# Two memsets moved behind the warm matmuls at the start of an attention and feed-forward kernel

## The chip, the cores and the metric

One core of a Trainium2 chip runs the whole program. The metric is the device time of one execution in microseconds. Before the change it is 955.84 us in the median of three runs (953.73 to 956.58); the profiled execution took 955.52 us.

## The reference

Three stages follow each other on 4 batches, 8 heads, 576 positions and a head width of 64; q, k, v and the output are float32, the weights 64-bit floats:

```
scores = q k^T / 8 + ALiBi bias, only where 0 <= i - j < 128
attn   = softmax(scores) v                 -> x [2304, 512]
x      = ((x w_a) * (x w_b)) w_out         (inner width 1536)
out    = ((x w1) * (x w2)) w3 w_out2       (inner width 1024)
```

The window of 128 means that a block of 128 query rows needs only its own block of keys and the one before it.

## The kernel before

The feed-forward products need float32 accuracy. Each factor is split into two `fp32r` parts, high and low (`hi` and `lo`), and three products (`lo` by `hi`, `hi` by `lo`, `hi` by `hi`) are summed in PSUM. The weights are loaded as pairs of integers (`raw`) and converted: ScalarE takes the absolute value of the upper word (`L113`, into `ca`) and a function of the lower word (`L116`, into `ce`), VectorE does four passes with shifts and masks (`L120`, `L123`, `L127`, `L132`), then `split` writes the high part on ScalarE (`L141`) and the low part on VectorE (`L78`). One such chain converts a block of 128 x 512 weights.

Attention runs in steps of one batch, one run of query blocks (blocks 0 and 1, blocks 2 and 3, block 4) and one pair of heads. For each block, `prep` transposes q and k on TensorE (`L287`, PSUM tiles `tr`) and ScalarE copies them out (`L296` into `w_q` and `w_k`, `L302` into `last_q` and `last_k`). A step then has: the scores (`L341`, tiles `s`), bias and row minimum on VectorE (`L368`, tile `pe`), the exponential on ScalarE (`L374`), the transposition of the weights (`L406`) and its copy (`L273` on ScalarE, `L275` on VectorE, tile `pt`), the product with v (`L428`), the division (`L434`, `L450`, `L452`) and the split of the result into `x_hi` (`L457`, ScalarE) and `x_lo` (VectorE). The four head pairs of the first run complete `x` for the first 256 tokens: four `x_hi`, the fourth for the last head pair.

In the gaps of attention, a `Filler` places the first feed-forward products (`g1`, matmuls at `L589`). Their first group needs the first 256 tokens of `x` and the first converted weight blocks. The conversions themselves are handed out one stage at a time by `side.turn()`.

What sets the order: TensorE's instructions are written by hand from the attention loop on (`manual_schedule` for PE). The instructions of the other engines, and TensorE's before that loop, are put in order when the program is built, by a simulated timeline (`schedule_with_timeline_sim=True`). Each engine works through its own list in order and waits at the first instruction whose inputs are missing. All loads are issued by SyncE's queue; the order of its first entries is: q and k of block 0, q and k of block 1, v twice, q and k of block 2 (`early`), further q, k and v, then the first two blocks of w_a and w_b.

At the start VectorE clears `last_q` and `last_k` (`L794`, `L795`), then in `consts` the tiles `pad`, `q_last` and `k_t`, and last `warm` (`L811`), a tile of zeros on which ten matmuls without use run (`keep_warm`, `L396`). `last_q` and `last_k` hold the last, half block of q and k of batch 0; their cleared parts are read by the scores of that block.

Of the kernel before, what the change touches and what calls it, by code (L numbers as in the profile page):

```python
# [44 lines left out]
def attention_moe_moe(ctx, tc, q, k, v, w_a, w_b, w_o, w_1, w_2, w_3, w_o2, out):  # L45
    nc = tc.nc
# [3 lines left out]
    P = 128  # L50
# [3 lines left out]
    LAST = S - (NB - 1) * P  # L54
# [337 lines left out]
    def keep_warm(cnt, x):  # L392

        ps = mm_tile(W)
        for y in range(cnt):
            nc.tensor.matmul(ps[:, :x.shape[1]], x[:, 0:P], x, start=(y == 0), stop=(y == cnt - 1))  # L396
# [69 lines left out]
    def mm_tile(n):  # L466
        ps = pools["mm"]
        turn[0] += 1
        return ps[turn[0] % len(ps)].tile([P, n], F32, name="mm")
# [321 lines left out]
    ys = ExitStack()  # L791
    y_p = ys.enter_context(tc.tile_pool(name="y_p", bufs=1, side="right"))
    last_t = [y_p.tile([P, NP, (1 + x) * P], F32, name=f"last_{'qk'[x]}") for x in range(2)]
    nc.vector.memset(last_t[0], 0.0)  # L794
    nc.vector.memset(last_t[1][:, :, P + LAST:], 0.0)  # L795
    pools["gate"] = gate_pa
    pools.update(abufs=1, gbufs=2)

# [11 lines left out]
    fl = Filler()  # L810
    nc.vector.memset(warm, 0.0)  # L811
    keep_warm(10, warm[:, 0:2 * P])
    paid = 0.0
    fixed = ExitStack()
    fixed.enter_context(tc.manual_schedule(engines={mybir.EngineType.PE}))
# [65 lines left out]
```

## Time and profile before

| | |
|---|---|
| median of three runs | 955.84 us |
| profiled execution | 955.52 us |
| its span, first to last instruction | 953.7 us |
| TensorE matmuls busy | 935.6 us |
| VectorE busy | 541.0 us |
| ScalarE busy | 421.7 us |
| mean granted TensorE clock | 0.996 |

The span is what the trace covers; the execution's own time is 1.8 us longer. The averages hide that the first 44 us look different from the rest: in a row of busy time by stretch, each engine's busy time stands behind the length of the stretch, and the granted clock of TensorE near the end (1.00 is 2.4 GHz, 0.50 is 1.2 GHz). In the rows of a timeline an instruction's duration reaches a little into the next one of the same engine, because the engine overlaps the end of one with the start of the next.

### The profile page before, as it was taken

The page shows a single profiled execution, that of the slowest core. Times are in us where ns is not written, and L with a number is a line of the kernel's source. Part 1 is how long each engine was busy: PE and PEld are TensorE (multiplying, and loading weights), DVE is VectorE, ACT ScalarE, POOL GpSimd, SP SyncE. Part 2 cuts the span into 40 slices and gives each one's busy share as a digit, 9 for nine tenths or more (in the row PEclk, how much of TensorE's full clock was granted, in tenths as well). Part 3 has the DMA queues.
Part 4 walks back from the last instruction along what each step waited for, and adds up shares of the span by engine and source line. Part 5 has one row for each costly group of instructions (what it writes and reads, how often), then busy time and mean ns, then how long its engine had stood idle before and what let it go on. Part 6 is the DMA issues. An engine that isn't in the chain of part 4 may idle for free.

```text
span 953.7 us, 13991 instructions
## 1 busy us (share of the span) xinstructions
PE 935.6 (98%) x5350; PEld 782.4 (82%) x5350; DVE 541.0 (57%) x1283; ACT 421.7 (44%) x952; POOL 157.8 (17%) x139
## 2 busy tenths in 40 slices
PE   7899999999999999999999999999999999999998
PEld 5687878878888888888888888888888888888886
DVE  5979787837995456675735744813822822522222
ACT  6978787845753245344524432433421411311111
POOL 3000000011112111120111111355211112111111
PEclk9999999999999999999999999999999999999999
DMA  9633333004441223132412320300300300000112
GB/s 231 140 79 73 80 72 73 2 1 154 134 133 56 89 94 105 67 121 79 152 36 78 122 67 17 117 1 1 118 15 1 126 7 1 23 1 1 44 59 97
DMA packets 90371, 68.28 MB, mean 72 GB/s; under 512 B 58304, under 2 KB 79296, under 8 KB 90304
## 3 DMA queue, kind: packets, MB, share of 16 engines
q1 hardware_dynamic: 90304, 67.38, 24.6%
q8 instruction: 42, 0.69, 0.3%
q14 instruction: 25, 0.20, 0.1%
HBM read 58.20 MB, written 8.91 MB: 70 GB/s over the span
## 4 chain that ended last, share of the span: by engine, by line
PE 92%; DVE 4%; ACT 3%; issue 1%; DMA 0%; POOL 0%; DVEq 0%
PE mm L589 51%; PE mm L641 13%; PE mm L657 10%; PE mm L493 5%; PE tr L428 3%; PE s L341 2%; PE mm L617 2%; PE tr L406 2%; ACT pe L374 2%; PE tr L287 2%; DVE pe L368 1%; DVE pe L388 1%; PE mm L485 1%; PE mm L629 1%; DMA early<-in_q 0%
## 5 line engine op out<-in xcount | busy, mean ns | idle before, releaser
L78 POOL TENSOR_TENSOR gl<-g,gh 128x512 fp32r<-128x512 f32 (+1 forms) x102 | 125.2, 1228 | 779.2 <-ACT gh L601 779.2
L598 DVE TENSOR_TENSOR g<-a,mm 128x512 f32<-128x512 f32 (+1 forms) x102 | 63.4, 621 | 201.9 <-PE mm L589 200.9
L601 ACT ACTIVATE gh<-g 128x512 fp32r<-128x512 f32 (+1 forms) x102 | 59.0, 579 | 149.2 <-DVE g L598 148.8
L596 ACT ACTIVATE a<-mm 128x512 f32<-128x512 f32 (+1 forms) x102 | 55.2, 542 | 121.5 <-PE mm L589 121.5
L589 PE MATMUL mm<-x_hi,wlA 128*128 128x512 f32 (+1 forms) x416 | 102.9, 369 | 2.8 <-ACT x_hi L457 2.8
L589 PE MATMUL mm<-x_lo,whA 128*128 128x512 f32 (+1 forms) x416 | 100.2, 363 | 0.1
L589 PE MATMUL mm<-x_hi,whA 128*128 128x512 f32 (+1 forms) x416 | 100.0, 363 | 0.0
L589 PE MATMUL mm<-x_lo,whB 128*128 128x512 f32 (+1 forms) x400 | 98.7, 368 | 0.0
L589 PE MATMUL mm<-x_hi,wlB 128*128 128x512 f32 (+1 forms) x400 | 98.6, 368 | 0.0
L589 PE MATMUL mm<-x_hi,whB 128*128 128x512 f32 (+1 forms) x400 | 98.1, 368 | 0.0
L116 ACT ACTIVATE ce<-raw,pad 128x512 int32<-128x512 uint32 x76 | 57.8, 761 | 64.8 <-DVE ca L132 32.1
L589 PEld LDWEIGHTS mm<-x_hi,wlA 128*128 128x128 f32 x416 | 71.6, 190 | 15.3 <-ACT x_hi L457 3.0
L589 PEld LDWEIGHTS mm<-x_lo,whA 128*128 128x128 f32 x416 | 73.0, 190 | 12.5 <-DVE x_lo L78 0.3
L589 PEld LDWEIGHTS mm<-x_hi,whA 128*128 128x128 f32 x416 | 73.3, 191 | 12.0
L589 PEld LDWEIGHTS mm<-x_hi,wlB 128*128 128x128 f32 x400 | 71.2, 188 | 12.7
L589 PEld LDWEIGHTS mm<-x_lo,whB 128*128 128x128 f32 x400 | 71.1, 189 | 12.5
L589 PEld LDWEIGHTS mm<-x_hi,whB 128*128 128x128 f32 x400 | 71.0, 189 | 12.5
L645 DVE TENSOR_TENSOR acc<-acc,mm 128x512 f32<-128x512 f32 (+1 forms) x100 | 62.0, 629 | 32.9 <-PE mm L641 32.7
L374 ACT ACTIVATE pe<-pe,st 128x256 f32<-128x256 f32 (+1 forms) x144 | 68.5, 478 | 12.2 <-DVE st L368 11.6
L113 ACT ACTIVATE ca<-raw 128x512 f32<-128x512 f32 x76 | 50.8, 668 | 51.5 <-DMA raw<-in_moe_w 24.8
L132 DVE SCALAR_TENSOR_TENSOR ca<-ce,ca 128x512 int32<-128x512 int32 x76 | 56.3, 740 | 12.0 <-ACT ce L116 10.2
L127 DVE SCALAR_TENSOR_TENSOR ca<-raw,ca 128x512 int32<-128x512 int32 x76 | 60.9, 802 | 1.8
(137 smaller groups left out, 1543.9 us busy)
## 6 DMA issues: line engine op xcount, KB each, us to landing
raw<-in_moe_w SPq DMA_DIRECT2D x32, 512.0 KB, 3.6
raw<-in_moe_w_out SPq DMA_DIRECT2D x20, 512.0 KB, 3.5
raw<-in_moe_w_a SPq DMA_DIRECT2D x12, 512.0 KB, 3.6
raw<-in_moe_w_b SPq DMA_DIRECT2D x12, 512.0 KB, 3.6
out<-acc SPq DMA_DIRECT2D x18, 256.0 KB, 2.0
v<-in_v SPq DMA_DIRECT2D x16, 256.0 KB, 4.0
w<-ce SPq DMA_DIRECT2D x16, 256.0 KB, 2.0
raw<-w SPq DMA_DIRECT2D x16, 256.0 KB, 2.8
```

What stands on the lines that cost most here:

```text
L78: eng.tensor_tensor(out=out, in0=a, in1=b, op=ALU.subtract)
L116: nc.scalar.activation(e, lw, ACTF.Relu, bias=seven, scale=-(2.0 ** -29))
L127: nc.vector.scalar_tensor_tensor(out=ai, in0=hw, scalar=-(1 << 30), in1=ai, op0=ALU.bitwise_and, op1=ALU.bitwise_or)
L132: nc.vector.scalar_tensor_tensor(out=ai, in0=es[0], scalar=7, in1=ai, op0=ALU.bitwise_xor, op1=ALU.bitwise_or)
L374: nc.scalar.activation(pe[:, j, :n], pe[:, j, :n], ACTF.Exp, bias=st[:, 0, j:j + 1], scale=-1.0, accum_out=st[:, 1, j:j + 1],)
L589: nc.tensor.matmul(p, w[:, z, kk, :], x[:, kk], start=(y == 0), stop=(y == len(terms) - 1))
L596: nc.scalar.activation(a, ps[0], ACTF.Copy)
L598: nc.vector.tensor_tensor(out=gg, in0=a, in1=ps[1], op=ALU.mult)
L601: nc.scalar.activation(gh, gg, ACTF.Copy)
L641: nc.tensor.matmul(p, w, x, start=(y == 0), stop=(y == len(terms) - 1))
L645: nc.vector.tensor_tensor(out=ya, in0=ya, in1=p, op=ALU.add)
L657: nc.tensor.matmul(p, x, w, start=(y == 0), stop=(y == len(terms) - 1))
```

## The change

The two memsets of `last_q` and `last_k` stand in the text behind the memset of `warm` and the ten warm matmuls, instead of ahead of `consts`.

```
     last_t = [y_p.tile([P, NP, (1 + x) * P], F32, name=f"last_{'qk'[x]}") for x in range(2)]
-    nc.vector.memset(last_t[0], 0.0)
-    nc.vector.memset(last_t[1][:, :, P + LAST:], 0.0)
     pools["gate"] = gate_pa
...
     nc.vector.memset(warm, 0.0)
     keep_warm(10, warm[:, 0:2 * P])
+    nc.vector.memset(last_t[0], 0.0)
+    nc.vector.memset(last_t[1][:, :, P + LAST:], 0.0)
     paid = 0.0
```

Line numbers after the change: `warm` is cleared at `L809`, the two tiles at `L811` and `L812`; all other lines named here keep theirs. The built order changes on TensorE at the start, on VectorE and ScalarE over their first 130 and 83 rows, and on SyncE in one place, where the first load of w_out is issued one entry sooner, ahead of a q load. GpSimd's order is the same, and behind these rows nothing is moved.

TensorE, at the start of the program; `tr` are the transposed q and k, `warm` is the tile of zeros:

```order
 L877 UNCONDITIONAL_BRANCH
-L287 MATMUL tr<-ident,early 128x128 x4
 L396 LDWEIGHTS warm
 L396 MATMUL mm<-warm 128x256
```

```order
 L396 LDWEIGHTS warm
 L396 MATMUL mm<-warm 128x256
-L287 MATMUL tr<-ident,early 128x128 x12
+L287 MATMUL tr<-ident,early 128x128 x16
 L341 MATMUL s<-w_k,w_q 128x128 x2
 L341 MATMUL s<-w_k,w_q 128x256 x2
```

The four transposes of the first tile have moved behind the ten warm matmuls, to the other twelve.

ScalarE, in the third and fourth steps of attention, before the change; `raw_241`, `raw_243` and `raw_247` are the first block of w_a, the first of w_b and the second of w_a, `DMAHW4_49` to `DMAHW6_49` their loads:

```order
L374 ACTIVATE pe_329,st_328<-pe_329,st_328 128x128 [waits DVE_49]
L374 ACTIVATE pe_334,st_328<-pe_334,st_328 128x256 [waits DVE_49]
L450 ACTIVATE r_389<-tr_339 128x256 [waits PE_49]
L296 ACTIVATE w_q_116<-tr_354 128x4x128 [waits PE_49]
L273 ACTIVATE pt_371<-tr_366 128x512 [waits PE_49]
L457 ACTIVATE x_hi_67<-y_391 128x256 [waits DVE_49]
L113 ACTIVATE ca_251<-raw_241 128x512 [waits DMAHW4_49]
L116 ACTIVATE ce_253<-raw_241,pad_73 128x512
L374 ACTIVATE pe_403,st_402<-pe_403,st_402 128x128 [waits DVE_49,Activation_49]
```

The same place with the change:

```order
L374 ACTIVATE pe_329,st_328<-pe_329,st_328 128x128 [waits DVE_49]
L113 ACTIVATE ca_251<-raw_241 128x512 [waits DMAHW4_49]
L116 ACTIVATE ce_253<-raw_241,pad_73 128x512
L374 ACTIVATE pe_334,st_328<-pe_334,st_328 128x256 [waits DVE_49]
L450 ACTIVATE r_389<-tr_339 128x256 [waits PE_49]
L296 ACTIVATE w_q_116<-tr_354 128x4x128 [waits PE_49]
L113 ACTIVATE ca_260<-raw_243 128x512 [waits DMAHW5_49]
L273 ACTIVATE pt_371<-tr_366 128x512 [waits PE_49]
L113 ACTIVATE ca_311<-raw_247 128x512 [waits DMAHW6_49,Pool_49]
L457 ACTIVATE x_hi_67<-y_391 128x256 [waits DVE_49]
L374 ACTIVATE pe_403,st_402<-pe_403,st_402 128x128 [waits DVE_49,Activation_49]
```

The conversions of three weight blocks begin five to eight rows sooner, ahead of an exponential, of `r` and of the first `x_hi`.

ScalarE, around the fourth `x_hi` (`x_hi_67<-y_605`), before the change; `raw_258` and `raw_309` are the two blocks of w_out, `pe_617` and `pe_622` belong to the next step:

```order
L457 ACTIVATE x_hi_67<-y_605 128x256
L374 ACTIVATE pe_617,st_616<-pe_617,st_616 128x256
L113 ACTIVATE ca_385<-raw_258 128x512
L374 ACTIVATE pe_622,st_616<-pe_622,st_616 128x256
L374 ACTIVATE pe_617,st_616<-pe_617,st_616 128x256
L374 ACTIVATE pe_622,st_616<-pe_622,st_616 128x256
L116 ACTIVATE ce_387<-raw_258,pad_73 128x512
L141 ACTIVATE whA1_245<-ca_376 128x512
L113 ACTIVATE ca_451<-raw_309 128x512
```

With the change:

```order
L273 ACTIVATE pt_590<-tr_585 128x512
L113 ACTIVATE ca_451<-raw_309 128x512
L116 ACTIVATE ce_387<-raw_258,pad_73 128x512
L141 ACTIVATE whA1_245<-ca_376 128x512
L374 ACTIVATE pe_617,st_616<-pe_617,st_616 128x256
L374 ACTIVATE pe_622,st_616<-pe_622,st_616 128x256
L457 ACTIVATE x_hi_67<-y_605 128x256
L374 ACTIVATE pe_617,st_616<-pe_617,st_616 128x256
L374 ACTIVATE pe_622,st_616<-pe_622,st_616 128x256
```

Five instructions that stood behind the fourth `x_hi` now stand right ahead of it; the sixth, `L113` on `raw_258`, stands ten rows further up.

## Rows read from the trace of the kernel before

**Rows 1.** The page's first part: busy time of each engine.

```profile
PE 935.6 (98%) x5350; PEld 782.4 (82%) x5350; DVE 541.0 (57%) x1283; ACT 421.7 (44%) x952; POOL 157.8 (17%) x139
```

**Rows 2.** Busy time in four stretches, then granted clock, DMA share, GB/s.

```profile
core 0: us, PE busy (x) PEld busy (x) DVE busy (x) ACT busy (x) POOL busy (x), PEclk, DMA share, GB/s
14.00:38.00 24.00, 19.72 (x177) 13.33 (x176) 21.04 (x84) 23.94 (x73) 0.00 (x0) 1.00 1.09 256
36.00:38.00 2.00, 0.32 (x2) 0.32 (x3) 2.00 (x9) 2.00 (x6) 0.00 (x0) 1.00 0.83 139
38.50:42.00 3.50, 3.48 (x16) 3.48 (x17) 2.96 (x7) 3.50 (x11) 0.00 (x0) 0.51 0.00 1
44.00:64.00 20.00, 20.00 (x216) 17.01 (x214) 14.29 (x49) 16.03 (x44) 1.46 (x2) 1.00 0.35 74
```

**Rows 3.** Timeline at the fourth x_hi: start, duration, engine, line, idle and releaser.

```profile
37.23 0.40 ACT L457 ACTIVATE x_hi<-y 128x256 fp32r<-128x256 f32 x1
...
37.69 0.39 PE L589 MATMUL mm<-x_hi,wlA 128*128 128x256 f32 x1 [2.77 <-ACT x_hi L457]
```

**Rows 4.** TensorE's waits over the span: us in total, times, longest.

```profile
PE tr L406 <- DVE pe L388: 2.6, 2, 1.7
```

**Rows 5.** Timeline of VectorE at the start.

```profile
0.90 0.48 DVE L794 MEMSET last_q<- 128x512 f32 x1 [0.90 <-PEq L868]
1.38 0.27 DVE L795 MEMSET last_k<- 128x256 f32 x1
...
3.32 0.27 DVE L811 MEMSET warm<- 128x256 uint32 x1
```

**Rows 6.** Timeline of TensorE from 4 to 12 us.

```profile
4.22 1.09 PE L287 MATMUL tr<-ident,early 128*128 128x128 f32 x4 [4.22 <-DMA early<-in_q]
5.10 2.34 PE L396 MATMUL mm<-warm 128*128 128x256 f16 x10
7.24 1.78 PE L287 MATMUL tr<-ident,early 128*128 128x128 f32 x12
...
11.41 0.63 PE L287 MATMUL tr<-ident,early 128*128 128x128 f32 x4 [0.90 <-DMA early<-in_q]
```

**Rows 7.** Timeline of SyncE's queue: when four of the loads are issued.

```profile
2.87 0.89 SPq L252 DMA_DIRECT2D early<-in_k  x1
...
6.15 1.14 SPq L252 DMA_DIRECT2D early<-in_q  x1
...
13.43 0.61 SPq L88 DMA_DIRECT2D raw<-in_moe_w_a  x1
...
14.64 0.52 SPq L88 DMA_DIRECT2D raw<-in_moe_w_a  x1
```

**Rows 8.** The same four loads: KB each, us from issue to landing.

```profile
early<-in_k SPq DMA_DIRECT2D x1, 256.0 KB, 4.8
...
early<-in_q SPq DMA_DIRECT2D x1, 256.0 KB, 5.1
...
raw<-in_moe_w_a SPq DMA_DIRECT2D x1, 512.0 KB, 5.0
...
raw<-in_moe_w_a SPq DMA_DIRECT2D x1, 512.0 KB, 8.3
```

**Rows 9.** Timeline of ScalarE: exponentials and conversions.

```profile
17.53 0.50 ACT L374 ACTIVATE pe<-pe,st 128x256 f32<-128x256 f32 x1
...
18.03 0.37 ACT L450 ACTIVATE r<-tr 128x256 f32<-128x256 f32 x1
18.29 0.59 ACT L296 ACTIVATE w_q<-tr 128x512 f32<-128x512 f32 x1
18.77 0.59 ACT L273 ACTIVATE pt<-tr 128x512 f32<-128x512 f32 x1
...
19.55 0.68 ACT L113 ACTIVATE ca<-raw 128x512 f32<-128x512 f32 x1
20.12 0.77 ACT L116 ACTIVATE ce<-raw,pad 128x512 int32<-128x512 uint32 x1
...
26.05 0.64 ACT L141 ACTIVATE whA<-ca 128x512 fp32r<-128x512 f32 x1
```

More of the change, by code (lines that the diff above doesn't have):

```diff
@@ L793, in attention_moe_moe @@
     last_t = [y_p.tile([P, NP, (1 + x) * P], F32, name=f"last_{'qk'[x]}") for x in range(2)]
-    nc.vector.memset(last_t[0], 0.0)
-    nc.vector.memset(last_t[1][:, :, P + LAST:], 0.0)
     pools["gate"] = gate_pa
@@ L812, in attention_moe_moe @@
     keep_warm(10, warm[:, 0:2 * P])
+    nc.vector.memset(last_t[0], 0.0)
+    nc.vector.memset(last_t[1][:, :, P + LAST:], 0.0)
     paid = 0.0
```

## Prediction

> **What bounds the kernel now.** I read the page's totals first, then busy time by stretch, then the rows around the largest wait that is not a load, then the start. TensorE is busy in 98% of the span [rows 1], and from 44 to 64 us it has no gap at all [rows 2]: there only its own work counts, and whatever shifts its start of that stretch shifts the end. Before 42 us it is different. From 14 to 38 ScalarE is busy in 23.94 of 24 us and VectorE in 21.04; in 36:38 both are full, and TensorE has 0.32 us of work [rows 2]. So this front belongs to two engines that are full and work in order, and to loads. What ends it is the fourth `x_hi` (`L457`, the one of the last head pair) at 37.23: with it the first 256 tokens of the feed-forward input are complete, and the matmul that waited 2.77 us for it starts at 37.69 [rows 3].
>
> **The change part by part.** *The two memsets* take 0.48 and 0.27 us [rows 5]. The instructions stay, now after `warm`. VectorE is through with its memsets at 3.59, the scores that it works on next need transposes that end at 7.24 + 1.78 = 9.02 [rows 5, 6], and so they cost nothing in the new place.
>
> *TensorE's start.* `warm` was ready at 3.32 + 0.27 = 3.59; without 0.75 us in front of it, it is ready at 2.84 [rows 5]. The ten warm matmuls take 7.24 - 5.10 = 2.14 us [rows 6] and end near 5.0, where before four transposes ran first from 4.22 and the other twelve from 7.24. But transposes need loads: the fourth tile is issued at 2.87 and lands 4.8 later, at 7.67 [rows 7, 8]. Before, its transposes ended at 9.02. Now they start no sooner than 7.67 and need 0.88 us at the pace of the first four (5.10 - 4.22 [rows 6]) or half of that: they end at 8.1 to 8.6, 0.4 to 0.9 us earlier. The Trainium skill (TensorE: Matmul & The Clock Gate, What's actually happening) says that the array starts throttled and that activity releases it. By that rule the earlier warm block brings the shorter figure, 0.9. The sum is the same by either.
>
> What becomes of the 0.4 to 0.9 us? The next transposes wait for the fifth tile, issued at 6.15 and landed 5.1 later, at 11.25; TensorE already waits 0.90 us for it and goes on at 11.41 [rows 6 to 8]. Those loads wait for nothing that the change moves, so TensorE just waits longer. I take 0; the lower end is -0.9, if all of it got through.
>
> *The order behind it.* The larger part is not in the diff. ScalarE's and VectorE's instructions are ordered by a simulated timeline, and it moves the weight conversions forward. ScalarE's order shows two places; its distances from start to start are read in [rows 9]: `L374` on 256 columns 0.50, `L450` 0.26, `L296` 0.48, `L113` 0.57, and with a duration less the 0.11 by which such rows overlap the next (19.55 + 0.68 against 20.12) `L273` 0.48, `L116` 0.66, `L141` 0.53.
>
> First place: the `L113` and `L116` on `raw_241` (the first block of w_a) stood behind the exponentials of the third step, `r`, `w_q`, `pt` and the first `x_hi`. Now they stand ahead of the last of those exponentials. Their load is issued at 13.43 and lands 5.0 later, at 18.43 [rows 7, 8]. ScalarE got to that exponential at 17.53 [rows 9]. Being in order it stands for 18.43 - 17.53 = 0.90 us, with work behind it that was ready. If the head start above reaches it, it stands longer by as much; the instruction starts at 18.43 either way. So the front hangs on a load that the change does not move.
>
> Second place: from 18.43 ScalarE does `L113` 0.57, `L116` 0.66, `L374` 0.50, `L450` 0.26, `L296` 0.48, a second `L113` 0.57, `L273` 0.48: 3.52 us, to 21.95. Next comes the third `L113`, on `raw_247`, whose load is issued at 14.64 and lands 8.3 later, at 22.94 [rows 7, 8]. That is another 0.99 us of standing, with the first `x_hi` and the next exponentials behind it.
>
> Third: what stands ahead of the fourth `x_hi`. Before, `L113` on `raw_258` and `raw_309`, `L116` on `raw_258`, `L141` on `ca_376` and the first two exponentials of the next step came after it. Now all six come ahead of it: 2 x 0.57 + 0.66 + 0.53 + 2 x 0.50 = 3.33 us. ScalarE had no idle time to take this in [rows 2].
>
> Sum for the fourth `x_hi`: 0.90 + 0.99 + 3.33 = 5.22 us, so it starts at 37.23 + 5.2 = 42.4, and TensorE's wait of 2.77 us becomes about 8.
>
> *What is given back.* The 3.33 us of ScalarE's work are done earlier, so it is less behind after 42. But TensorE does not wait for it there: 20.00 of 20 us busy from 44 to 64 [rows 2]. The later waits for `pe` of `L388` come to 2.6 us in two places [rows 4]; each lies between a TensorE result and the next use of it, so it moves along with TensorE. I take nothing back; at most it is those 2.6.
>
> *The clock.* After the wait of 2.77 us the granted clock is 0.51 in 38.5:42, the 1.2 GHz level, and 1.00 from 44 on [rows 2]. That costs about half of 3.5 us, 1.7, and is already in the time before. I expect it once again after the longer wait, so no difference: bounds 0, and +1.7 for a second fall in the gaps that the two standing times open on TensorE between 18 and 28 us.
>
> *Sum*: 0 + 5.2 + 0 = +5.2 on the profiled execution of 955.52, whose span is 953.7 with 1.8 around it: **960.7 us**. The median of the runs is 955.84, 0.3 above that execution and inside their 953.73 to 956.58.
>
> **The rivals.**
> 1. *The start wins and the order is neutral.* It would be so if ScalarE's standing fell into time that was free anyway and the six instructions were not what `x_hi` waits for. For it: the start is what the edit's text moves. Against it: ScalarE's full stretch. It gives -0.9 to 0: 954.6 to 955.5.
> 2. *The front gets shorter* (the other side). If the conversions, being done sooner, let the fourth `x_hi` come 2.8 us earlier, TensorE's wait of 2.77 goes and with it the fall of the clock, 1.7: up to -4.5, 951.0. It is decided by `x_hi` coming before about 35 us. Against it: more work stands ahead of `x_hi` than before, not less.
> 3. *A second fall of the clock.* If it also falls in TensorE's gaps between 18 and 28, the work behind them runs at 1.2 GHz and the front is later by up to 1.7: 962.4. For it: the fall after 2.77 us [rows 2, 3]. Against it: ScalarE and VectorE carry the front there. The Trainium skill (the same page and section) states that idling brings the throttled level back; the trace agrees at 38.5, and by that rule this rival is the page's answer to the change.
> 4. *The cost is there but smaller.* If ScalarE reaches one or both loads when they have landed, or part of the 2.6 us of later waits shrinks: between +1 and +4, 956.5 to 959.5.
>
> **How the numbers follow.** A measurement of this kernel tells about 0.3% from no change, 2.9 us, so slower means above 958.7 and faster below 953.0. The forecast (+4 to +6, 959.5 to 961.5) has 0.50, rival 3 0.15, rival 4 0.17, rival 1 0.10, rival 2 0.08. Slower: 0.50 + 0.15 + 0.07 of rival 4, whose top 0.8 us lie above the bound, = 0.72. Within 0.3%: the other 0.10 of rival 4 and rival 1, 0.20. Faster: 0.08. The range reaches down over rival 4 and the upper end of rival 1 (a start that gains nothing) to 955.5, and up over rival 3, with one microsecond for VectorE's share of the moved work, to 963.4; rival 2 and half of rival 1, 0.13, stay outside.
>
> **What would show it.** Right: ten warm matmuls from about 2.9, the second step's scores still at about 12, an idle ScalarE ended by a load at 18.4 and again at 22.9, a matmul of `L589` that waits some 8 us for `x_hi` near 42.5, and from there the old trace shifted by 5 us. Wrong: if ScalarE shows no wait at those two loads, my landing times don't hold; if `x_hi` comes late but the shift at 200 us is much smaller, the work done early was given back; if the wait at `L589` is shorter than 2.8 us, rival 2 holds.

## The result and the profile after

The changed kernel takes 961.31 us in the median of six runs (957.95 to 963.67), before 955.79 in as many (953.73 to 956.58): ratio 1.0061, 95% interval 1.0039 to 1.0083; the medians lie 5.5 us apart. The forecast was 960.7 in 955.5 to 963.4. The profiled execution of the changed kernel took 960.29 us with a span of 958.5. TensorE's total row of the page answers to [rows 1]:

```profile
PE 937.7 (98%) x5350; PEld 784.0 (82%) x5350; DVE 542.0 (57%) x1283; ACT 421.9 (44%) x952; POOL 157.4 (16%) x139
```

No engine has more instructions, and TensorE's busy time is 2.1 us longer. So of the 4.8 us that the span grew, 2.7 are waiting, and the rest is the same work at a lower clock (mean granted clock 0.993, before 0.996). The timeline of TensorE at the start answers to [rows 6]:

```profile
2.83 2.32 PE L396 MATMUL mm<-warm 128*128 128x256 f16 x10 [2.83 <-DVE warm L809]
4.94 2.63 PE L287 MATMUL tr<-ident,early 128*128 128x128 f32 x12
7.83 0.66 PE L287 MATMUL tr<-ident,early 128*128 128x128 f32 x4 [0.26 <-DMA early<-in_k]
...
11.53 1.09 PE L287 MATMUL tr<-ident,early 128*128 128x128 f32 x4 [1.65 <-DMA early<-in_q]
```

The warm matmuls come first, the fourth tile's transposes end at 8.49 instead of 9.02, and the wait for the fifth tile grows from 0.90 to 1.65 us. The start gained half a microsecond and lost it at that load. But the four transposes behind it take 1.09 us, before 0.63. The rows by stretch (busy time of each engine, then granted clock) answer to [rows 2] and say why:

```profile
11.00:17.00 6.00, 5.47 (x26) 4.18 (x28) 2.55 (x15) 4.15 (x17) 0.00 (x0) 0.50 1.30 222
14.00:38.00 24.00, 21.19 (x182) 14.69 (x180) 20.65 (x79) 22.37 (x67) 0.00 (x0) 0.93 1.09 250
...
41.00:44.00 3.00, 0.97 (x4) 0.98 (x5) 2.66 (x7) 3.00 (x12) 0.00 (x0) 0.56 0.00 0
44.00:48.00 4.00, 4.00 (x21) 4.00 (x20) 2.32 (x5) 1.85 (x4) 0.00 (x0) 0.50 0.00 0
```

From 11 to 17 us the granted clock is 0.50, the 1.2 GHz level. Before it is 1.00 there, as the row of before shows:

```profile
11.00:17.00 6.00, 5.46 (x49) 3.92 (x51) 4.14 (x27) 5.79 (x22) 0.00 (x0) 1.00 1.29 219
```

Between 11 and 64 us only 38.5:42 is low before; here the clock is low a second time from 41 to 48. ScalarE's timeline at the two loads answers to [rows 9], and the last two rows to [rows 3]:

```profile
18.41 0.40 ACT L374 ACTIVATE pe<-pe,st 128x128 f32<-128x128 f32 x1 [0.90 <-DVE st L368]
...
19.69 0.67 ACT L113 ACTIVATE ca<-raw 128x512 f32<-128x512 f32 x1
...
23.21 0.67 ACT L113 ACTIVATE ca<-raw 128x512 f32<-128x512 f32 x1
...
42.54 0.43 ACT L457 ACTIVATE x_hi<-y 128x256 fp32r<-128x256 f32 x1
...
43.03 0.58 PE L589 MATMUL mm<-x_hi,wlA 128*128 128x256 f32 x1 [4.33 <-ACT x_hi L457]
```

ScalarE has no wait for a load: it comes to `raw_241` only at 19.69, behind scores that a slow TensorE delivered late, and to `raw_247` at 23.21. Both loads have landed by then, at 18.55 and 21.56 (issued at 13.55 and 14.76, 5.0 and 6.8 us to landing). The fourth `x_hi` starts at 42.54, 5.31 later than before (forecast 5.22). The first transposes behind the group that waits for it (`L406`) start at 49.34, before at 43.60; first the row of the changed kernel, then the one of before:

```profile
49.34 1.04 PE L406 MATMUL tr<-ident,pe 128*128 128x128 f32 x8
```

```profile
43.60 1.03 PE L406 MATMUL tr<-ident,pe 128*128 128x128 f32 x8
```

From there the trace is the old one, shifted: the first `L657` matmul starts at 681.1, before at 676.4.

Two accounts fit so far. By the **order**, the loss is ScalarE's and VectorE's new order. By the **clock**, it is the early start, which lets TensorE run dry until its clock falls.

### The profile page after: what moved, and what is told of

It is laid out like the page before. It is cut to its first block, busy times and chain, and to the rows that moved or that the text cites. A ratio compares the mean times of both kernels' runs of the same rounds, so it can differ in the third digit from the quotient of the medians.

```text
span 958.5 us, 13988 instructions
## 1 busy us (share of the span) xinstructions
PE 937.7 (98%) x5350; PEld 784.0 (82%) x5350; DVE 542.0 (57%) x1283; ACT 421.9 (44%) x952; POOL 157.4 (16%) x139
## 4 chain that ended last, share of the span: by engine, by line
PE 91%; ACT 4%; DVE 3%; issue 1%; SPq 1%; DMA 1%; POOL 0%; ACTq 0%; DVEq 0%
PE mm L589 51%; PE mm L641 13%; PE mm L657 10%; PE mm L493 5%; PE tr L428 3%; PE s L341 2%; ACT pe L374 2%; PE mm L617 2%; PE tr L406 2%; PE tr L287 2%; DVE pe L388 1%; PE mm L485 1%; DVE pe L368 1%; PE mm L629 1%; SPq L252 1%
## 5 line engine op out<-in xcount | busy, mean ns | idle before, releaser
L589 PE MATMUL mm<-x_hi,wlA 128*128 128x512 f32 (+1 forms) x416 | 103.4, 370 | 4.3 <-ACT x_hi L457 4.3
L589 PE MATMUL mm<-x_lo,whA 128*128 128x512 f32 (+1 forms) x416 | 100.2, 363 | 0.0
L589 PE MATMUL mm<-x_hi,whA 128*128 128x512 f32 (+1 forms) x416 | 100.2, 363 | 0.0
L589 PE MATMUL mm<-x_lo,whB 128*128 128x512 f32 (+1 forms) x400 | 98.7, 368 | 0.0
L589 PE MATMUL mm<-x_hi,wlB 128*128 128x512 f32 (+1 forms) x400 | 98.6, 368 | 0.0
L589 PE MATMUL mm<-x_hi,whB 128*128 128x512 f32 (+1 forms) x400 | 98.1, 368 | 0.0
L589 PEld LDWEIGHTS mm<-x_hi,wlA 128*128 128x128 f32 x416 | 72.0, 191 | 16.9 <-ACT x_hi L457 4.5
L589 PEld LDWEIGHTS mm<-x_lo,whA 128*128 128x128 f32 x416 | 73.3, 191 | 12.2
L589 PEld LDWEIGHTS mm<-x_hi,whA 128*128 128x128 f32 x416 | 73.3, 191 | 12.1
L589 PEld LDWEIGHTS mm<-x_hi,wlB 128*128 128x128 f32 x400 | 71.2, 188 | 12.7
L589 PEld LDWEIGHTS mm<-x_lo,whB 128*128 128x128 f32 x400 | 71.1, 189 | 12.5
L589 PEld LDWEIGHTS mm<-x_hi,whB 128*128 128x128 f32 x400 | 71.0, 189 | 12.5
L113 ACT ACTIVATE ca<-raw 128x512 f32<-128x512 f32 x76 | 50.7, 668 | 51.4 <-DMA raw<-in_moe_w 23.0
L368 DVE CUSTOM_DVE_ANT_0 pe<-s,relb 128x256 f32<-128x256 f32 (+1 forms) x144 | 49.3, 390 | 23.6 <-PE s L341 23.3
```

What stands on the lines that cost most here:

```text
L368: nc.vector.tensor_tensor_reduce(out=pe[:, j, :n], in0=ps[j], in1=bias, scale=-1.0 / float(D) ** 0.5, scalar=3.0e38, op0=ALU.add, op1=ALU.min,
L589: nc.tensor.matmul(p, w[:, z, kk, :], x[:, kk], start=(y == 0), stop=(y == len(terms) - 1))
```

## Experiments

The ratio of each kernel is to the kernel before, measured beside it, with its 95% interval. In every kernel here the order of the first 80 or 82 instructions of ScalarE and the first 96 to 112 of VectorE is held as a list, so that one edit doesn't move what another is to test. No kernel holds the lists of before and changes nothing else; experiments 2, 5 and 7 lie at 1.0000 to 1.0007 with lists held, so no cost of holding them is seen:

```
+    def pin(engine, order):
+        mine = [i for i in nc.cur_bb.bb.instructions if i.engine == engine and "Boundary" not in type(i).__name__]
+        mine = [mine[r] for r in order]
+        for a, b in zip(mine, mine[1:]):
+            tc.add_manual_dep(b, a.name, ...)
+    pin(mybir.EngineType.Activation, ACT_ORDER)
+    pin(mybir.EngineType.DVE, DVE_ORDER)
```

**1. The order alone.** The text of before, both lists from the changed kernel.

```
+ACT_ORDER, DVE_ORDER = (those of the changed kernel)
```

> The text of before (memsets ahead, transposes before the warm matmuls), with ScalarE's first 80 and VectorE's first 96 instructions held in the order that they have in the changed kernel. The order theory: TensorE starts as in before, its clock stays at 1.00 from 11 to 17 us, ScalarE reaches the two loads early and stands 0.9 us at 18.4 and up to 1.0 us at 22.9, and 3.3 us of extra work lie ahead of the fourth x_hi, which starts near 42.4 (at least 40.5, if the two standing times turn out to be free): +3.3 to +5.2 us on the whole, ratio 1.0035 to 1.0054. The clock theory (the loss comes from TensorE starting its warm block early and then waiting for the fifth load at a falling clock): no fall at 11 us, so only the part of the loss that is extra work, or less: fourth x_hi at most at 40.5 and a ratio of at most 1.0035; by its strong form, in which the order is hidden, no change, 1.000.

Measured: 1.0049 [1.0036, 1.0061]. Clock in two stretches and the two rows at the fourth `x_hi`:

```profile
11.00:17.00 6.00, 5.67 (x41) 3.63 (x39) 3.90 (x26) 5.14 (x20) 0.00 (x0) 1.00 1.29 229
...
27.00:30.00 3.00, 3.00 (x21) 1.91 (x21) 3.00 (x15) 3.00 (x8) 0.00 (x0) 0.50 1.22 246
...
41.22 0.41 ACT L457 ACTIVATE x_hi<-y 128x256 fp32r<-128x256 f32 x1
...
41.68 0.58 PE L589 MATMUL mm<-x_hi,wlA 128*128 128x256 f32 x1 [3.67 <-ACT x_hi L457]
```

Most of the loss is here, with a full clock from 11 to 17 and the old order at the start. `x_hi` is 4.0 us later than before. ScalarE did not stand at the loads here: it came to the first at 18.19, which is 0.66 later than the 17.53 of before (the twelve transposes at 7 us take 2.77 us in this execution, before 1.78), and to the third `L113` at 21.67. From 18.19 it needs 23.03 us to the fourth `x_hi`, before 19.70 from the same place: 3.33 more, the forecast's third term. So the standing times are not tested here. The clock does fall, but later, from 26 to 30 us, behind a wait of 1.65 us for `w_k`; ScalarE is busy in all of 27:30, and what this fall is worth is worked out further down.

**2. The start alone.** The text of the changed kernel, both lists from before.

```
+ACT_ORDER, DVE_ORDER = (those of before)
```

> The text of the changed kernel (warm matmuls first, memsets behind them), with ScalarE's first 80 and VectorE's first 96 instructions held in the order that they have in before. The order theory: the start alone costs nothing, the fourth x_hi starts near 37.2 and the ratio is 0.999 to 1.001. The clock theory: the granted clock is near 0.5 from 11 to 17 us as in the changed kernel, scores and exponentials come 2.2 us later, the fourth x_hi starts near 39.4: +2.2 us, ratio 1.0023; its strong form puts all of the loss here, +5, 1.0055.

Measured: 1.0006 [0.9996, 1.0016].

```profile
11.00:17.00 6.00, 5.47 (x36) 4.12 (x38) 2.77 (x18) 4.97 (x19) 0.00 (x0) 0.72 1.29 218
...
38.34 0.43 ACT L457 ACTIVATE x_hi<-y 128x256 fp32r<-128x256 f32 x1
```

The clock did fall here, from 12 to 16 us, and `x_hi` came 1.1 us later. Over twelve runs that is 0.6 us, inside the uncertainty. The interval excludes the 1.0023 of the clock account as well as the 1.0055 of its strong form, though the fall in this execution was shorter than in the changed kernel.

**3. The clock kept up at 11 us.** Twelve more warm matmuls in the changed kernel, behind the first scores.

```
+            if n == 0:
+                ops.append(hold)
...
+    def hold():
+        for _ in range(2):
+            keep_warm(6, warm[:, 0:2 * P])
...
```

> The changed kernel, with twelve more warm matmuls of 256 columns on TensorE behind the first scores, in the 1.65 us in which it waits for the fifth load; the orders of ScalarE and VectorE held. The granted clock should stay near 1.00 from 11 to 17 us. The order theory: the 2.2 us of slow start go, but ScalarE then reaches the first block of w_a before its load has landed and stands 0.9 us at 18.4 and 1.0 at 22.9 in its place: the fourth x_hi still near 42.4, ratio to before 1.004 to 1.006. If the slow clock alone made the second part of the loss: ScalarE has no such standing time, the fourth x_hi comes 2.2 us earlier, near 40.4, and the ratio falls to about 1.0033.

Measured: 1.0067 [1.0055, 1.0079]. ScalarE's rows at the two loads and the fourth `x_hi`, and a stretch:

```profile
18.48 0.69 ACT L113 ACTIVATE ca<-raw 128x512 f32<-128x512 f32 x1 [0.91 <-DMA raw<-in_moe_w_a]
...
22.77 0.68 ACT L113 ACTIVATE ca<-raw 128x512 f32<-128x512 f32 x1 [0.68 <-DMA raw<-in_moe_w_a]
...
42.25 0.42 ACT L457 ACTIVATE x_hi<-y 128x256 fp32r<-128x256 f32 x1
...
27.00:30.00 3.00, 2.50 (x13) 1.33 (x13) 2.40 (x11) 3.00 (x7) 0.00 (x0) 0.57 1.23 237
```

With the clock up at 11 us, both standing times of the prediction appear (0.90 and 0.99 were forecast), and `x_hi` starts within 0.3 us of where it did at the low clock. The 40.4 and 1.0033 that the clock account expected are refuted. In this execution the slow clock and the two loads cover each other. That holds as long as the second load is late: it landed at 22.68 here, at 21.23 in experiment 4. The clock fell here too, from 27 to 30 us.

**4. The clock kept up behind 38 us.** Forty warm matmuls in the changed kernel, ahead of the first group of `L589`.

```
+                if not began[0]:
+                    hold()          # 2 x keep_warm(20, ...)
                 began[0] = True
```

> The changed kernel, with forty more warm matmuls of 256 columns on TensorE just ahead of its first matmul of L589, which fill the wait of 4.3 us for the fourth x_hi; the orders of ScalarE and VectorE held. They change nothing of the time at which x_hi is ready (42.5), only TensorE's activity ahead of it. If the clock's fall behind that wait costs time, the granted clock stays near 1.00 from 43 to 48 us and half of 5.2 us come back: 2 to 2.6 us less than the changed kernel, ratio to before 1.003 to 1.004. If the fall costs nothing, since other engines are late there, the ratio stays at 1.006.

Measured: 1.0036 [1.0023, 1.0049], 959.10 us against 961.31. Three rows: TensorE's wait for the fifth tile, ScalarE at the first load, and a stretch.

```profile
11.41 0.63 PE L287 MATMUL tr<-ident,early 128*128 128x128 f32 x4 [1.66 <-DMA early<-in_q]
...
18.31 0.66 ACT L113 ACTIVATE ca<-raw 128x512 f32<-128x512 f32 x1 [0.86 <-DMA raw<-in_moe_w_a]
...
44.00:48.00 4.00, 4.00 (x35) 3.81 (x35) 1.70 (x3) 2.27 (x5) 0.73 (x1) 1.00 0.00 0
```

The medians lie 2.2 us apart, but the intervals of the two ratios overlap, and in this execution a part has another cause: `x_hi` starts at 41.19 and not at 42.54, since the clock is up at 11 us and the second load has landed when ScalarE comes to it at 21.80. What the fall behind the long wait is worth is read from the rows of experiment 5. The first row shows more: up to there this kernel is the changed one, it waits the same 1.66 us, and here the transposes behind it take 0.63 us. So the fall at 11 us doesn't always come with this wait.

**5. The six instructions put back.** The changed kernel, its orders held up to the third `x_hi`, the orders of before from there, on VectorE too (its list is not shown).

```
-ACT_ORDER = [..., L113 raw_258, x_hi 3, ..., L113 raw_309, L116 raw_258, L141 ca_376, L374, L374, x_hi 4, ...]
+ACT_ORDER = [..., x_hi 3, ..., x_hi 4, L374, L113 raw_258, L374, ..., L116 raw_258, L141 ca_376, L113 raw_309, ...]
```

> The changed kernel with its orders held up to the third x_hi, and from there the rest of the 80 and 116 instructions of ScalarE and VectorE in the order of before: the six instructions (3.33 us) that came ahead of the fourth x_hi stand behind it again, all else of the change stays. The order theory: the fourth x_hi starts 3.3 us earlier than in the changed kernel, near 39.2 (38 if the clock does not fall at 11 us and one load is waited for), and the ratio to before falls to 1.002 to 1.003. The rival, that the six are not what x_hi waits for: still near 42.5 and 1.006.

Measured: 1.0007 [0.9996, 1.0017]. The loss is gone, more of it than expected. TensorE and ScalarE in order of time:

```profile
11.23 0.63 PE L287 MATMUL tr<-ident,early 128*128 128x128 f32 x4 [1.64 <-DMA early<-in_q]
...
39.14 0.38 PE L589 MATMUL mm<-x_hi,wlA 128*128 128x256 f32 x1 [1.04 <-ACT x_hi L457]
...
43.30 1.03 PE L406 MATMUL tr<-ident,pe 128*128 128x128 f32 x8
```

```profile
18.14 0.66 ACT L113 ACTIVATE ca<-raw 128x512 f32<-128x512 f32 x1 [0.87 <-DMA raw<-in_moe_w_a]
...
22.62 0.69 ACT L113 ACTIVATE ca<-raw 128x512 f32<-128x512 f32 x1 [0.88 <-DMA raw<-in_moe_w_a]
...
38.68 0.40 ACT L457 ACTIVATE x_hi<-y 128x256 fp32r<-128x256 f32 x1
```

ScalarE stands at both loads, 1.75 us, and `x_hi` is 1.45 us later than before. But TensorE, late itself, waits only 1.04 us for it, the clock stays at 1.00, and `L406` starts at 43.30, 0.3 earlier than before. From the matmul that waits to `L406` TensorE takes 4.16 us at the full clock, before 43.60 - 37.69 = 5.91 and in the changed kernel 49.34 - 43.03 = 6.31: the fall there costs 1.75 and 2.15 us. So in this execution the clock that is kept pays for the two loads. From its arrival at the first load ScalarE needs 38.68 - 18.14 - 0.88 = 19.66 us to the fourth `x_hi` without standing, as before (19.70): the six instructions carry the loss. SyncE's load that moved with the order stays moved in this kernel, so it is not the cause.

**6. The loads not waited for.** The kernel of experiment 3, the conversions of the two loads further back.

```
-ACT_ORDER = [..., L113 raw_241, L116 raw_241, L374, r, w_q, L113 raw_243, pt, L113 raw_247, x_hi 1, ...]
+ACT_ORDER = [..., L374, r, w_q, pt, L113 raw_241, L116 raw_241, L113 raw_243, x_hi 1, L374, L374, L116 raw_243, L113 raw_247, ...]
```

> The changed kernel with the twelve warm matmuls at 10 us (so that TensorE is on time), and with the conversions of the two loads at 18.4 and 22.9 us put far enough back in ScalarE's order, and their VectorE steps with them, that the loads have landed; the six instructions ahead of the fourth x_hi stay. The order theory with its full sum: the 0.91 and 0.68 us of standing go, the fourth x_hi starts 1.6 us earlier than in the kernel with the twelve warm matmuls alone, near 40.7, and the ratio to before falls from 1.0067 to 1.005. The rival, that VectorE or TensorE were as late and the standing was free: 42.2 and 1.006 to 1.007.

Measured: 1.0079 [1.0064, 1.0094], a miss by both accounts. ScalarE's rows, then one of TensorE and a stretch:

```profile
22.64 0.76 ACT L116 ACTIVATE ce<-raw,pad 128x512 int32<-128x512 uint32 x1 [0.39 <-DVE ca L132]
...
28.60 0.76 ACT L116 ACTIVATE ce<-raw,pad 128x512 int32<-128x512 uint32 x1 [0.63 <-DVE ca L132]
...
42.07 0.41 ACT L457 ACTIVATE x_hi<-y 128x256 fp32r<-128x256 f32 x1
```

```profile
45.30 0.58 PE L589 MATMUL mm<-x_lo,whA 128*128 128x256 f32 x1 [1.54 <-DVE x_lo L78]
...
27.00:30.00 3.00, 3.00 (x21) 1.92 (x21) 3.00 (x14) 2.37 (x6) 0.00 (x0) 0.50 1.26 254
```

The two waits for loads are gone. In their place ScalarE waits 1.02 us for VectorE's later conversion steps, and TensorE waits another 1.54 us for `x_lo`. The clock is also low for nine microseconds here, from 26 to 35. What the standing times alone are worth at the end stays open: this edit does not take them away without a substitute, and it comes with a longer fall.

**7. The fourth x_hi earlier than before.**

```
-ACT_ORDER = [..., L374, pt, L116 raw_249, L141 ca_311, pt, x_hi 4, ...]
+ACT_ORDER = [..., L374, x_hi 4, pt, L116 raw_249, L141 ca_311, pt, ...]
```

> The kernel before, its orders held, with one instruction of ScalarE moved up: the fourth x_hi stands right behind the exponentials that close its step, ahead of pt (two times L273), L116 and L141; on VectorE its x_lo stands ahead of one conversion step. The order theory says that the end of the front is where the fourth x_hi stands in ScalarE's order: it starts 2.1 us earlier, near 35.1, TensorE's wait at L589 shrinks from 2.8 to at most 0.9 us and the clock does not fall behind it: 2.1 to 3.9 us less, ratio 0.996 to 0.998. The rival: what was put behind x_hi is needed by TensorE just as soon (the transposes of probabilities and the second weight tile), so the wait only moves to them: ratio 0.999 to 1.001.

Measured: 1.0000 [0.9992, 1.0009]. The rows at `x_hi`, and the stretch behind:

```profile
35.26 0.40 ACT L457 ACTIVATE x_hi<-y 128x256 fp32r<-128x256 f32 x1
...
35.72 0.39 PE L589 MATMUL mm<-x_hi,wlA 128*128 128x256 f32 x1 [0.65 <-ACT x_hi L457]
...
44.00:64.00 20.00, 18.07 (x185) 15.09 (x186) 14.72 (x56) 15.64 (x47) 1.46 (x2) 1.00 0.35 74
```

All that was to happen at 35 us did: the wait shrank to 0.65, the clock stayed up, and `L406` starts at 40.34, 3.3 us sooner. Then TensorE waits 1.93 us in the stretch from 44 to 64, for `pt` and `y`, where before it had no gap: there it stands behind ScalarE and VectorE. At its wait for `pe` at 131 us 0.8 of the 3.3 us are left (130.76 against 131.54), and in the ratio nothing. The order account expected 0.996 to 0.998 and missed; its rival, that the wait only moves, held. A late `x_hi` is paid for, an early one is not rewarded.

**8. The clock kept up in before, once and twice.** 28 warm matmuls ahead of the first group of `L589`; in a second kernel also 14 at 206 us; in a third those 14 with the edit of experiment 7.

```
+                if not began[0]:
+                    hold()          # 2 x keep_warm(14, ...)
                 began[0] = True
```

> The kernel before, its orders held, with 28 warm matmuls of 256 columns on TensorE ahead of its first matmul of L589, which fill the wait of 2.8 us for the fourth x_hi. x_hi stays at 37.2. If the fall of the clock from 38.7 to 42.0 costs time, the clock stays near 1.00 and 1.2 to 1.7 us come back, ratio 0.998 to 0.9988. If the other engines bind there, 1.000.

> The kernel before, its orders held, with 28 warm matmuls ahead of its first matmul of L589 (as in the run before) and 14 more at 206 us, ahead of the first matmul of L617 that waits there for gh (0.42 us) and gl (0.62 us); behind those two waits the granted clock fell to 0.5 for some 3.5 us in the profiled runs of before and of three others, and not in those of the changed kernel and of four others. If such falls are chance and cost 1.5 us each, this kernel has neither fall: 953.0 to 953.6, ratio 0.997 to 0.998, and its runs lie closer together than those of before. If the fall at 206 us costs nothing in the median, as with the one hold: 0.9987.

> The kernel before with the fourth x_hi moved up in ScalarE's order (as in the run that had it alone) and the 14 warm matmuls at 206 us. With x_hi early TensorE was 3.3 us ahead at 40 us and 1.0 us at 676 us. If the fall at 206 us is what took part of it: 953 to 954, ratio 0.997 to 0.9985. If ScalarE and VectorE set the pace up to 60 us and take all of it back, and the fall at 206 us is chance in both kernels: 955.0, ratio 0.9995 to 1.000.

Measured: 0.9987 [0.9978, 0.9995] with one hold, 0.9989 [0.9981, 0.9998] with two, 1.0011 [1.0001, 1.0020] in the third. The first is a little faster than before, at a median of 953.91 us against 955.54. The second hold brings nothing more in the median, but its twelve runs lie within 953.98 to 955.19, the 22 of before beside them in 954.04 to 957.17. The third missed both of its expectations: it is no faster than before and by its interval a little slower; why is open. An early `x_hi` is again worth nothing. TensorE's rows of the first at the fourth `x_hi`, then a stretch of the second:

```profile
35.15 3.23 PE L396 MATMUL mm<-warm 128*128 128x256 f16 x28
38.13 0.80 PE L589 MATMUL mm<-x_hi,wlA 128*128 128x256 f32 x4
```

```profile
132.00:136.00 4.00, 4.00 (x29) 3.19 (x28) 3.41 (x17) 2.21 (x9) 0.00 (x0) 0.58 0.08 19
```

In the first the front of the profiled execution was 0.85 us late (`x_hi` at 38.08 instead of 37.23), and `L406` still starts at 42.94, 0.66 sooner than before. In the second neither of the two falls that were held off came, but a third one did, at 132 us.

## Why the prediction was right, point by point

*The memsets and the start.* Right. The memsets lie in VectorE's free time, the fourth tile's transposes end at 8.49 (forecast 8.1 to 8.6), the fifth load takes the rest, and the start alone is 1.0006. Left out was what can happen to the clock behind a longer wait.

*The two standing times* (0.90 and 0.99). Right in part: 0.91 and 0.68, 0.86 and none, 0.87 and 0.88 in experiments 3 to 5, and none in experiment 1. The first load landed 4.9 to 5.0 us after its issue in all of these, as forecast; the second took 6.6 to 8.1 us, and the forecast used the 8.3 of one execution. In the profiled execution of the changed kernel neither standing time came, which the forecast had named as a sign that its landing times don't hold. The first did hold (18.55); ScalarE was 2.16 us late at `raw_241` (19.69 against 17.53) behind the fall of the clock at 11 us. That these 2.16 us are near the forecast 0.90 + 0.99 = 1.89, so that `x_hi` came within 0.1 us of the forecast in this execution, is luck.

*Rival 3* put a second fall of the clock between 18 and 28 us and on top of the sum, at up to 1.7 us. In the changed kernel the fall came at 11 us and in place of a part of the sum. A fall behind the wait for `w_k` near 26 us did come in experiments 1, 3, 4 and 6. In the first three ScalarE's way from the first load to the fourth `x_hi`, without standing, is 23.03, 23.09 and 22.88 us, in the changed kernel without that fall 22.85: this fall cost `x_hi` at most 0.24 us, as the forecast's argument against the rival has it (ScalarE carries the front).

*The 3.33 us ahead of `x_hi`.* Right, and the part that decides. From its arrival at `raw_241` ScalarE needs 42.54 - 19.69 = 22.85 us to the fourth `x_hi`, before 37.23 - 17.53 = 19.70 from the same place in the program: 3.15 more, and 3.18 to 3.39 more in experiments 1, 3 and 4. With 3.33 and the standing times seen, the forecast's sum gives 37.23 + 3.33 + 1.59 = 42.15 for experiment 3 (measured 42.25) and 41.42 for experiment 4 (41.19). Without the six, 37.23 + 1.75 = 38.98 for experiment 5 (38.68).

*TensorE's wait at `L589`* (forecast 8, measured 4.33). Wrong in size: TensorE came to it at 38.08 and not at 34.30, since its own work in the front was late by the same causes. It does not matter for the end, which follows `x_hi`.

*The clock behind the wait* (taken as unchanged, at 1.7 us). Nearly: it is low for some 7 us instead of 3.5, and for five of them TensorE works. `L406` is late by 5.74 where `x_hi` is late by 5.31, so that is 0.4 us. By the rows of experiment 5 the fall costs 2.15 us in the changed kernel and 1.75 in before; keeping the clock up in before brought 0.13% or 1.2 us (experiment 8, 0.5 to 2.1 by its interval).

*Nothing is given back.* Right. The waits for `pe` are the same 2.6 us as in [rows 4]:

```profile
PE tr L406 <- DVE pe L388: 2.6, 2, 1.7
```

The shift shrinks from 5.74 at `L406` to 4.7 at `L657`, but not by the order: before, the clock falls once more behind two short waits at `L617`, in the profiled execution of the changed kernel not, behind the same two. Ahead of them the shift is 213.40 - 207.56 = 5.84 us, behind them, at the next `L589`, 221.36 - 217.02 = 4.34. The two rows are of before and, 6 us later, of after:

```profile
209.00:213.00 4.00, 4.00 (x17) 2.85 (x18) 0.23 (x1) 1.09 (x3) 0.00 (x0) 0.57 0.00 0
```

```profile
215.00:219.00 4.00, 4.00 (x29) 2.82 (x29) 0.36 (x2) 1.75 (x5) 0.00 (x0) 1.00 0.00 0
```

*Rival 2* gave 951.0 if `x_hi` came early enough. Experiment 7 had that `x_hi` and gained nothing: the rival's price was wrong, not only its condition.

## What to carry to other kernels

Here an edit that moves two instructions cost 0.6% through the order that is rebuilt around it; compare the built orders before judging the edit, and count what now stands ahead of the one instruction that the busiest engine waits for. Test such a point in both directions: here a later `x_hi` cost its delay, an earlier one brought nothing, since TensorE then waited for other results of ScalarE and VectorE. Where a wait can't be removed, matmuls without use that fill it may pay, since the clock stayed up behind them here; 28 of them brought 0.13% (0.05 to 0.22).

## What the runs showed of the hardware

The same wait at the same place may or may not bring the lower clock: 1.65 us at 11 us did in the changed kernel, 1.66 and 1.64 us there did not in experiments 4 and 5, nor did a wait of 2.63 us for `w_k` at 27 us in experiment 5. Waits of 1.64 to 2.43 us for the same `w_k` did in experiments 1, 3, 4 and 6, and one of 1.66 us in the changed kernel did not. Two waits of 0.42 and 0.62 us near 210 us were followed by a fall in the profiled run of before and of experiments 2, 3, 6 and 7, and by none in the changed kernel, in experiments 1, 4 and 5 and in the first kernel of experiment 8. The wait of 1.71 us for `pe` near 131 us is in all twelve traces and was followed by a fall in one, the second kernel of experiment 8. The Trainium skill (TensorE: Matmul & The Clock Gate, What's actually happening) says that idling brings the throttled level back; these runs agree that it can, and show that the length of one wait does not tell whether it will. All of this is read from one profiled execution of each kernel.

The result of every run has its mean granted clock, and the times go with it: in the changed kernel it is 0.996 in the shortest run (957.95 us) and 0.991 in the three longest (961.59 to 963.67); of the 22 runs of before beside experiment 8 the seven with 0.998 took 954.04 to 955.36, the three with 0.995 took 956.72 to 957.17. I take such falls to be why the runs of the changed kernel spread over 5.7 us and those of before over 2.9 us; shown of that is only that the spread is narrower with two holds, 1.2 us in twelve runs.
